# Hash attention and a gelu feed-forward on one core: another order of the start, and a later mark for GpSimd's sums

## The chip, the cores and the metric

The kernel runs on one core of a Trainium2 chip. Its engines have instruction streams of their own: TensorE (PE, with its weight loads as PEld), VectorE (DVE), ScalarE (ACT), GpSimd (POOL) and SyncE (SP). SP and ACT issue most of the transfers. The metric is the device time in microseconds of one execution.

## The reference

Two blocks follow each other. First attention over 4 batches of 8 heads, 768 positions, 64 elements a head, in which a query sees only the keys that fall in its own bucket; the bucket is the six signs of the row times a projection. Then a feed-forward block over the 3072 tokens.

```python
q_bits = (np.einsum('bhsd,dk->bhsk', q, proj) > 0).astype(np.int64)
k_bits = (np.einsum('bhsd,dk->bhsk', k, proj) > 0).astype(np.int64)
mask = q_bucket[:, :, :, None] == k_bucket[:, :, None, :]
scores = np.where(mask, scale * np.matmul(q, k.transpose(0, 1, 3, 2)), -1000000000.0)
attn = np.exp(scores - max);  attn = attn / (sum + 1e-09)
x = np.matmul(attn, v)          # heads side by side: 3072 x 512
h = x @ w_in                    # 512 -> 2048
g = h * (1.0 / (1.0 + np.exp(-1.702 * h)))
out = g @ w_out                 # 2048 -> 512
```

The inputs q, k, v and proj are float32; the two weights are float64 and are turned into float32 on the chip.

## The kernel before, in words

**Order.** The instructions of TensorE, VectorE, ScalarE and GpSimd keep the order in which the program writes them (`manual_schedule`, line 72). Only SP's transfers are placed by the framework: a transfer of SP goes ahead as early as its tile and its semaphores allow. Transfers on ACT and GpSimd stand in those engines' own order.

**Attention** (lines 286 to 618) goes over 16 pairs of heads (4 batches, 4 pairs). For a pair it has q and k turned (features on the partitions), and sign features of the bucket bits as bfloat16. `scores` (426) makes for each of 6 key tiles one product of features, which puts a large negative number where the buckets differ, and one float32 product of q and k into the same PSUM bank; ScalarE takes the exponential. `add_low` on GpSimd and `add_high` on VectorE add the exponentials for the denominators; `values` (453) multiplies by v; `total`, `invert` and `norm` divide.

**The first pair** (`first_pair`, 345) has its own path, as nothing is there to hide its loads. SP and ACT ask for half of k each, then for the projections `pj` (two copies, on partitions 0 to 63 and 64 to 127, line 357), then for q. TensorE warms with four products of a zero tile `idle` (362). `hash_weights` (123) makes hash weights of `pj` on VectorE: four small products for k and one copy into the padded `pf0`, then the same for q. `turned` (365) turns half of k or q by products with `ident` into a PSUM tile `tp`, which VectorE or ScalarE copies to kT or qT. `bits` (373) makes the signs of one half: a product with `pf0` into PSUM (`hash0`), and a comparison on VectorE into the features kf or qf. `measure` (396) sums squares on ScalarE, for a guard. The order is: turn k first half, k second half, q first half, q second half; bits of k first half, q first half, k second half; then the first scores; the bits of the second half of q come behind the first three key tiles. The PSUM tiles of `tp` and `hash0` come from the pool of the scores, which has three buffers.

**Conversion of w_in** (`convert`, 158). Chunks of 512 columns come in as raw float64 bits (`raw`, 512 KB each, one buffer), and VectorE and ScalarE make float32 of them, one chunk in each pair's iteration from pair 2 on. `begin` (517) makes a chunk's generator and asks for its transfer; `step` (514) goes on with it. The helper `behind` (316) is a memset of one column on VectorE: a transfer into that tile then waits for it.

**Feed-forward** (698 on). Both products use seven-product block schemes (Strassen-Winograd), nested once, so that sums of operand quarters stand ahead of the products and sums of results behind them. The second product has 21 output steps (`steps_out`, 1022: three blocks of tokens by seven outer products). In an output step `product_of_halves` (1066) makes seven products of halves, 2 x 4 float32 passes of 256 columns each, in the order 1, 2, 3, 6, 7, 5, 4, and VectorE adds them up. Four operand sums of the next step, `g_sums` (1044: t1, t2, d12, t4), run on VectorE between those additions. The sums of w_out's quarters, `inner_sums` (1015), run on GpSimd, for the first seven steps alone. Their start is held by `mark`, a copy of one element on GpSimd, in steps 2, 3, 5 and 6 (1233): GpSimd goes on when that element has been written. In the trace the L1077 products of steps 1, 2, 3 and 4 start at 605.90, 617.99, 630.08 and 642.65 us.

The lines of the change:

## Time and profile before

| | us |
|---|---|
| median of 3 runs | 859.48 |
| lowest and highest | 858.7, 860.01 |
| the profiled execution | 858.67 |
| its span | 856.8 |
| TensorE busy | 846.2 |
| VectorE busy | 703.3 |
| GpSimd busy | 353.4 |
| ScalarE busy | 344.9 |
| first scores' product starts | 10.80 |
| last product ends | 848.3 |

The page gives busy times by engine, the chain of work that ended last, and groups of instructions. A row of the order of time has start, duration, engine, line, operation, result and operands, shape and count, and in brackets the engine's idle time before it and what ended it. A float32 matmul appears as two records, one for each pass.

### The profile page before, as it was taken

How to read it: one execution, taken by the hardware profiler on the slowest of the kernel's cores; microseconds unless marked ns; L12 is line 12 of the kernel's file. 1: busy time of each engine (PE TensorE's matmuls, PEld its weight loads, DVE VectorE, ACT ScalarE, POOL GpSimd, SP SyncE). 2: the span in 40 equal slices, each digit the busy share in tenths (PEclk: the TensorE clock that was granted, in tenths of full speed). 3: DMA queues.
4: the chain of work that ended last, by engine and by line, in shares of the span. 5: the costliest groups of instructions: out<-in, count | busy, mean ns of one | idle time of the engine just before them, and what ended most of it. 6: DMA issues, size and time to landing. Idle time of an engine off the chain costs nothing.

```text
span 856.8 us, 13648 instructions
## 1 busy us (share of the span) xinstructions
PE 846.2 (99%) x5007; PEld 529.2 (62%) x5007; DVE 703.3 (82%) x1072; ACT 344.9 (40%) x549; POOL 353.4 (41%) x316
## 2 busy tenths in 40 slices
PE   9999999999999999999999999999999999999996
PEld 4444444444444444566666666545888888888885
DVE  4589999999999885788987788577998977797776
ACT  5866667777666654343444444433000000000000
POOL 4343333433433359996854476669725000000000
PEclk9999999999999999999999999999999999999999
DMA  5625755445563104436555546587745685467524
GB/s 131 101 47 107 113 89 85 85 86 99 115 97 71 47 26 150 144 134 233 194 204 217 221 153 234 202 278 257 275 151 190 192 254 197 155 191 245 197 99 101
DMA packets 160987, 132.11 MB, mean 154 GB/s; under 512 B 122608, under 2 KB 137616, under 8 KB 155536
## 3 DMA queue, kind: packets, MB, share of 16 engines
q1 hardware_dynamic: 152016, 106.63, 45.0%
q10 hardware_dynamic: 8896, 24.53, 8.3%
q8 instruction: 41, 0.67, 0.3%
q14 instruction: 34, 0.28, 0.1%
HBM read 79.69 MB, written 50.33 MB: 152 GB/s over the span
## 4 chain that ended last, share of the span: by engine, by line
PE 96%; DVE 2%; DMA 1%; ACT 0%; issue 0%; ACTq 0%; SPq 0%; DVEq 0%
PE product L1077 28%; PE product L751 22%; PE ps L435 18%; PE av L468 15%; PE small L819 6%; PE product L819 3%; PE dn L489 1%; PE hash L411 1%; DVE xT L1081 1%; DVE y L1057 1%; DMA pj<-in_proj_dram 1%; PE hash L376 0%; DVE v L1081 0%; DVE raw_g L223 0%; DVE t2a L224 0%
## 5 line engine op out<-in xcount | busy, mean ns | idle before, releaser
L436 ACT ACTIVATE e<-ps 128x768 f32<-128x768 f32 x192 | 151.2, 812 | 25.7 <-PE ps L435 23.1
L435 PE MATMUL ps<-qT,kT 64*128 64x384 f32 x768 | 155.1, 482 | 0.0
L443 POOL TENSOR_TENSOR acc<-e 128x768 f32<-128x768 f32 x32 | 51.8, 1617 | 193.8 <-ACT e L436 174.3
L468 PE MATMUL av<-e,v 128*32 128x385 f32 x1536 | 128.0, 487 | 0.0
L751 PE MATMUL product<-xT,w_in_sb 128*128 128x512 f32 x216 | 100.1, 593 | 0.1
L468 PEld LDWEIGHTS av<-e,v 128*32 128x32 f32 x1536 | 48.5, 109 | 76.2 <-issue 74.6
L435 PEld LDWEIGHTS ps<-qT,kT 64*128 64x128 f32 x768 | 68.0, 187 | 38.5 <-issue 38.4
L751 PE MATMUL product<-t_x,s_in 128*128 128x512 f32 x192 | 89.4, 592 | 0.0
L1090 ACT COPY u<-product 128x256 f32<-128x256 f32 x21 | 7.8, 372 | 172.2 <-PE product L1077 139.0
L751 PEld LDWEIGHTS product<-xT,w_in_sb 128*128 128x128 f32 x216 | 40.9, 190 | 36.5 <-issue 33.0
L435 PE MATMUL ps<-qf,kf 64*128 64x384 bf16 x384 | 62.9, 324 | 0.1
L444 POOL TENSOR_TENSOR acc<-acc,e 128x768 f32<-128x768 f32 x32 | 55.8, 1744 | 2.5
L751 PEld LDWEIGHTS product<-t_x,s_in 128*128 128x128 f32 x192 | 36.5, 190 | 29.7 <-issue 26.8
L449 DVE SCALAR_TENSOR_TENSOR acc<-e 128x768 f32<-128x768 f32 x32 | 47.7, 1490 | 5.1 <-ACT e L436 5.1
L767 DVE TENSOR_TENSOR u<-product,u 128x256 f32<-128x256 f32 (+1 forms) x60 | 28.4, 486 | 16.4 <-PE product L819 13.2
L435 PEld LDWEIGHTS <-kf 64*128 64x128 bf16 x384 | 18.9, 94 | 35.1 <-issue 6.2
L451 DVE TENSOR_TENSOR acc<-acc,e 128x768 f32<-128x768 f32 x32 | 34.3, 1072 | 3.3
L451 DVE TENSOR_TENSOR acc<-acc,acc 128x768 f32<-128x768 f32 x32 | 31.2, 974 | 6.3 <-POOL acc L444 3.2
L1077 PE MATMUL product<-raw_g,xT 128*128 128x256 f32 x152 | 35.1, 379 | 0.0
L222 POOL TENSOR_TENSOR u<-v,u 128x1024 f32<-128x1024 f32 (+1 forms) x11 | 23.9, 2168 | 21.9 <-ACT v L764 8.1
L767 DVE TENSOR_TENSOR v<-product,v 128x512 f32<-128x512 f32 x24 | 16.5, 689 | 19.4 <-PE product L751 19.4
L767 DVE TENSOR_TENSOR c<-small,c 128x256 f32<-128x256 f32 (+1 forms) x54 | 24.1, 460 | 8.8 <-PE small L819 8.6
(278 smaller groups left out, 1727.3 us busy)
## 6 DMA issues: line engine op xcount, KB each, us to landing
raw_g<-g_dram SPq DMA_DIRECT2D x22, 1024.0 KB
s_in<-g_dram SPq DMA_DIRECT2D x20, 1024.0 KB
g_dram<-c ACTq DMA_DIRECT2D x18, 512.0 KB
raw<-in_moe_w_out_dram ACTq DMA_DIRECT2D x16, 512.0 KB
raw<-in_moe_w_in_dram SPq DMA_DIRECT2D x15, 512.0 KB
v<-in_v_dram SPq DMA_DIRECT2D x32, 192.0 KB
k<-in_k_dram SPq DMA_DIRECT2D x60, 96.0 KB
q<-in_q_dram SPq DMA_DIRECT2D x60, 96.0 KB
```

What stands on the lines that cost most here:

```text
L222: return [lambda: eng.tensor_tensor(t1, b12, b11, op=Alu.subtract), lambda: eng.tensor_tensor(b12, b22, b12, op=Alu.subtract), lambda: eng ...
L435: nc.tensor.matmul(ps[:, j, 0:HS], a[hs, keys], m[hs, cols], start=not last, stop=last)
L436: nc.scalar.activation(es[c][:, kt, :, 0:HS], ps[:, :, 0:HS], Act.Exp, scale=1.0 / D**0.5)
L443: nc.gpsimd.tensor_tensor(acc, es[c][:, 0, :, 0:HS], es[c][:, 1, :, 0:HS], op=Alu.add)
L444: nc.gpsimd.tensor_tensor(acc, acc, es[c][:, 2, :, 0:HS], op=Alu.add)
L449: nc.vector.scalar_tensor_tensor(acc, e[0], T * TINY, e[1], op0=Alu.add, op1=Alu.add)
L451: nc.vector.tensor_tensor(acc, acc, x, op=Alu.add)
L468: nc.tensor.matmul(av[D * j + d : D * j + d + 32, :], vt[:, t, j, d : d + 32], es[c][:, t, j, :], start=(t == 0), stop=(t == T - 1))
L751: nc.tensor.matmul(ps, wq[LEFT[i]][:, kc, :], xq[RIGHT[i]][:, kc, :], start=(start and kc == 0), stop=(kc == K2 - 1), skip_group_check=not ...
L767: nc.vector.tensor_tensor(dst, x, y, op=Alu.add)
L819: nc.tensor.matmul(x, wq[LEFT[i]], xq[RIGHT[i]], start=start, stop=True, skip_group_check=True)
L1077: nc.tensor.matmul(ps, wq[LEFT[i]][:, c, :], gq[RIGHT[i]][:, c, :], start=(c == 0), stop=(c == F4 - 1))
```

## The change

Four edits:

- The projections are asked for first of all in the program, by two transfers on GpSimd's queue, ahead of GpSimd's making of `ident`. The tile `idle` and its memset are gone; the warming products read a constant 1.0 in float32, of 256, 256, 256 and 128 columns.
- The first chunk's transfer is put behind a memset of `raw` on VectorE, which stands behind the features of pair 3. On SP it moves from behind the first loads of v to behind the feature writes of pair 3, ahead of the loads of k and q for pair 5.
- In the first pair, the first half of kT is copied by ScalarE instead of VectorE. The bits of both halves of k come first, then those of q's first half; the second half of q is turned behind them. The sum of squares of q moves ahead of the copy of that half on ScalarE. The `hash0` tiles of q come from another PSUM pool (`mps`).
- In the output steps 2 and 3 `mark` copies an element of t2 of that step, instead of an element of the results of the step before.

```diff
-    idle = const.tile([P, 512], BF16, name="idle")
-    nc.vector.memset(idle, 0.0)
+    pj = const.tile([P, NB], F32, name="pj")
+    for j in range(2):
+        nc.gpsimd.dma_start(out=pj[D * j : D * (j + 1)], in_=proj)
     ident = const.tile([P, P], F32, name="ident")
     make_identity(nc, ident)
...
-    def convert(cv, dst, src, queue=None, psum=None):
+    def convert(cv, dst, src, queue=None, psum=None, behind=None):
         raw = cv.tile([P, CW, 2], U32, tag="raw", name="raw")
+        if behind is not None:
+            behind(raw[:, 0, 0:1])
         (queue or loader[0]).dma_start(out=raw, in_=src)
...
-                    if i == 0:
-                        for j, queue in enumerate((nc.sync, nc.scalar)):
-                            queue.dma_start(out=pj[D * j : D * (j + 1)], in_=proj)
...
-                for _ in range(4):
-                    nc.tensor.matmul(aps.tile([P, 512], F32, tag="av", name="warm"), idle[:, 0:P], idle, start=True, stop=True)
+                for cols in (256, 256, 256, P):
+                    one = [nc.const_aps.tensor(1.0, [P, x], F32) for x in (P, cols)]
+                    nc.tensor.matmul(aps.tile([P, cols], F32, tag="av", name="warm"), *one, start=True, stop=True)
...
-                    h = sps.tile([P, 2, 512], F32, tag="s", name="hash0")[:, 0, 0:HS]
+                    if name == "q":
+                        h = mps.tile([P, HS], F32, tag="m", name="hash0")
+                    else:
+                        h = sps.tile([P, 2, 512], F32, tag="s", name="hash0")[:, 0, 0:HS]
...
-                turned("k", 0, nc.vector.tensor_copy)
+                turned("k", 0, nc.scalar.copy)
                 turned("k", 1, nc.vector.tensor_copy)
                 turned("q", 0, nc.scalar.copy)
-                turned("q", 1, nc.scalar.copy)
                 measure(0, "q")
                 bits("k", 0)
+                bits("k", 1)
                 bits("q", 0)
-                bits("k", 1)
+                turned("q", 1, nc.scalar.copy)
                 return lambda: bits("q", 1)
...
-                    conv[n] = convert(cv, *in_chunks[n - 2])
+                    conv[n] = convert(cv, *in_chunks[n - 2], behind=behind if n == 2 else None)
...
-                    nc.gpsimd.tensor_copy(mark, ms[OUTER[n - 1]][0:1, 0, 0:1])
+                    nc.gpsimd.tensor_copy(mark, (g_quarters(n)[5] if n < 4 else ms[OUTER[n - 1]])[0:1, 0, 0:1])
```

More of the change, by code (lines that the diff above doesn't have):

```diff
@@ L82 @@
     later = []
-    pj = const.tile([P, NB], F32, name="pj")
     def offsets(name, row):
```

## The prediction

> **What bounds the kernel now.** I read the page first (busy time, chain), then the chain at the start, the rows of the first pair's transposes, and the order of time around the one place where TensorE waits late.

> ```profile
> span 856.8 us, 13648 instructions
> PE 846.2 (99%) x5007; PEld 529.2 (62%) x5007; DVE 703.3 (82%) x1072; ACT 344.9 (40%) x549; POOL 353.4 (41%) x316
> PE 96%; DVE 2%; DMA 1%; ACT 0%; issue 0%; ACTq 0%; SPq 0%; DVEq 0%
> ```

> TensorE is the bound nearly everywhere: 846.2 of 856.8 us, 96% of the chain. An edit can pay only where TensorE stands still, or where it does filler. That leaves the start (first scores at 10.80 us), the tail behind the last product (848.3 to 856.8 us by VectorE and the last stores, not touched), and small holes. The chain of waits at the start:

> ```profile
> 1.20 4.38 DMA pj<-in_proj_dram
> ...
> 6.27 0.18 DVE pf_k L133
> ...
> 6.95 0.18 DVE pf_q L133
> 7.14 0.48 DVE kT L371
> 7.61 0.04 issue
> 7.66 0.88 PE tp L369 x12
> 8.54 1.50 PE hash L376 x4
> ...
> 10.13 0.63 DVE qf L377
> 10.76 0.04 issue
> 10.80 2.60 PE ps L435 x18
> ```

> Read it downwards: the projections, two transfers of 1.5 KB asked for at 1.20, land at 5.58 and hold VectorE. Eight small products and two copies into the weights (1.45 us) stand between them and the copies of kT. The last q transposes wait for the first copy to free their PSUM buffer (7.61), the hashes stand behind those transposes, and qf ends at 10.76. The page of one tile gives TensorE's two speeds:

> ```profile
> L369 PE MATMUL tp<-ident,k x24: 420/421/474, 3.8 to 6.3; 128*64 128x128 f32 x24
> L369 PE MATMUL tp<-ident,q x24: 272/273/472, 6.5 to 8.3; 128*64 128x128 f32 x24
> ```

> The same form takes 421 ns until 6.3 us and 273 ns after. By starts, 24 passes of k last 2.9 us (107 ns apart), and 12 of q 0.88 us (55 ns apart): the array runs at half rate up to about 6.5 us. The granted clock reads 1.00 all along, so only durations show it. Last, the order of time in the second half:

> ```profile
> 629.17 1.26 DVE L1081 TENSOR_TENSOR v<-v,xT 128x256 f32<-128x256 f32 x1
> ...
> 630.23 1.33 POOL L217 TENSOR_TENSOR w_in_sb<-xT,w_in_sb 128x512 f32<-128x512 f32 x1
> 630.36 1.95 DVE L1081 TENSOR_TENSOR xT<-xT 128x256 f32<-128x256 f32 x2
> ...
> 634.35 1.22 DVE L224 TENSOR_TENSOR t2b<-s_in,t1b 128x1024 f32<-128x1024 f32 x1
> ...
> 635.67 1.53 PE L1077 MATMUL product<-t2b,w_in_sb 128*128 128x256 f32 x6 [0.25 <-issue]
> ```
> ```profile
> 639.86 0.43 DVE L1081 TENSOR_TENSOR v<-v,xT 128x256 f32<-128x256 f32 x1
> ```

> The same addition takes 1.26 us beside POOL's sums and 0.43 without them. t2b comes at 635.57, and TensorE, which wanted it at 635.26 (starts 1.73 apart per product), begins at 635.67.

> **The change, part by part.** The sum is made against the profiled execution: 858.67 us, a span of 856.8 and 1.87 around it. That lies 0.81 below the median of the runs shown (859.48).

> *POOL's sums behind t2 (steps 2 and 3).* Nothing is added but a later wait. In step 2 the mark waited for the sum c11 (613.59) and its four sums ran from 613.7 to 619.1; in step 3 they ran from 626.3 to 631.6. Three additions between SBUF tiles took 1.41, 1.49 and 1.38 us there in step 2, and 1.26 and 1.49 in step 3, for 0.43 alone. Behind t2 these 2.9 and 1.9 us go, and t2b comes at about 633.7 or before, ahead of 635.26. TensorE gets back 0.41 us (635.67 less 635.26) and up to 0.07 of restart: I take 0.45, with 0 and 0.48 as ends. Queued behind the mark on POOL are the four sums, of which the later output step has need from 633.5 and 646.1 on. They would end at about 626 and 639, before both. What VectorE does next to them is late next: d12 and t4, alone 1.22 us, up to 2.28 beside POOL (the longest such row, t1b at 652.86). d12 of step 3 ends then by 636, for a product at 637.0; t4 by 638.7, for 640.5. Both are covered, by 1 us and more.

> *The start.* Projections: two transfers move from the two hardware queues to POOL's, ahead of ident. The ACT and SP queues lose 0.57 and 0.59 us of issue each, so q is asked for 0.6 us sooner (it was not late by more than that: first transpose of q at 6.46, when k's had ended). POOL has no transfer in this trace. Nearest rows: an issue takes 0.40 to 0.82 us on SP, and landing took 3.1 us (k: issue 0.73, first use 3.81) to 4.38 (pj). So pj lands between 0.73+0.8+3.1 = 4.6 and 0.73+1.64+4.38 = 6.75. I take 5.0, nearer to the first, as no other packets stand in that queue. It has to be there 0.78 us (the products for k) before the first hash. POOL's other memsets move back by 0.8 to 1.6: ident ended at 1.30 and is first used behind the warming; above_q ended at 2.94 and is used at 9; the last ended at 8.55, and POOL then idled 4.97 us. Hidden.

> Warming: 4 x 512 columns in bfloat16 become 896 columns in float32, started without a memset: about 0.85 instead of 1.19. By the hash rows, 384 columns in float32 take 0.645 us at full rate, so 896 take 1.5, or 3.0 at half rate. The four waits between cost 0.2 each (a warming product took 0.63, of which 0.43 is streaming at half rate). It ends at about 4.65, and k's transposes, at 3.81 before, start 0.85 later: this is a cost, paid back only because the old chain waited for pj anyway.

> From there TensorE works without a hole: 24 passes of k, 12 of q, three hashes (3 x 0.645), 0.16 of drain, 0.62 of qf with 0.1 of signals; the last q transposes run under qf. kT's first half goes to ACT (0.48), which has finished measuring k at 4.81, so no copy holds a hash. If the rate doubles at 6.5 as before: k until 6.9, q until 7.55, hashes until 9.5, scores at 10.4, against 10.80: 0.4 gained. If it doubles at 5.0, since TensorE starts sooner and is denser: k until 6.15, q until 6.8, hashes until 8.75, scores at 9.65: 1.15 gained. If it doubles at 8.0: scores at 11.1, 0.3 lost. I take 0.65, between the first two.

> [...]

> *First chunk later.* Its transfer moves on SP from 3.86 us to behind the feature writes that end at 63.0, ahead of the loads of k and q issued at 63.12 to 67.54. From rows: issue to landing 3.1 us (k, at the start) to 4.4, so 66.2 to 67.5; VectorE wants it at 67.37. At worst 0.1 late for six instructions whose results TensorE does not need for 200 us. The loads behind it come up to 2.5 us later (landed by 72.5, first used by VectorE at 80.1). One memset of 0.06 is added on VectorE. Taken at 0, ends 0 and 0.3. Without the slack at 80 it would cost its 2.5.

> Sum: 858.67 - 0.45 - 0.65 = 857.57, say **857.6**.

> **The rivals.**
> 1. *The warming eats the gain.* If the float32 weight loads (0.19 each at full rate) are not hidden, warming ends near 5.9 and scores start at about 11: the start loses 0.2, t2 still gives 0.45, so 858.4. Half-rate work until 8.0 gives the same, 858.5. For it: the warming ends after k has landed. Against it: loads lie under products everywhere else in this trace.
> 2. *Everything pays.* The rate doubles during the warming: 1.15 and 0.48, 857.0. For it: denser work, earlier. Against: the old warming, 2.5 us long, did not do it.
> 3. *POOL's queue is slow (slower than before).* The place is VectorE's wait for pj. Scores start 0.78+1.94+0.16+0.75 = 3.6 us behind pj's landing, so from 7.2 on the start loses, and from 9.4 on the whole is slower by over 0.2%; a landing at 10 gives 861.0. For it: no row bounds POOL's transfers, and ident stands behind their issue. Against: the rows' upper end is 6.75. [...]
> 4. *Nothing shows.* t2 was late only in this execution and the start is bound elsewhere: 858.7.

> **How the numbers follow.** Forecast 0.50, rival 1 0.20, rival 2 0.14, rival 3 0.11, rival 4 0.05. About 0.2% (1.7 us) is what a measurement of this kernel can tell from no change. The forecast is 0.22% under the median, 0.12% under the profiled execution, so it falls on either side of that line: I give three fifths of it to faster. Faster 0.30 + 0.14 = 0.44; within 0.20 + 0.20 + 0.05 = 0.45; slower 0.11. The range goes from rival 2 less 0.3 for the free instant of the clock, 856.7, to rival 1 with the median's 0.81 above its profile and the 0.5 by which runs lie above that, 859.8.

> **What would show it.** In the changed kernel's profile: pj from POOL landing before about 6; k's transposes starting at 4.5 to 4.9; three hashes in a row, and first scores at 9.6 to 10.5; additions next to the mark in steps 2 and 3 at 0.43 us; no idle time before the product that reads t2b; d12 or t4 longer than 1.22, with nobody waiting. Wrong it would be if the warming reaches past 5.5, if pj comes after 7, or if TensorE has a new hole between 620 and 645, or at 78 to 90, where the late loads are used.

## The result, and the profile after

| | before | after |
|---|---|---|
| median of 7 runs each, us | 858.71 | 861.81 |
| lowest and highest | 858.13, 860.01 | 860.97, 862.76 |
| ratio after / before, 95% interval | | 1.0033, 1.0021 to 1.0044 |
| profiled execution, its span | 858.67, 856.8 | 860.98, 859.1 |

The changed kernel is slower by 0.33%, outside the range of the prediction (856.7 to 859.8). The medians differ by 3.10 us, the two profiled executions by 2.30; that of after lies 0.83 below its median. The page of after:

```profile
span 859.1 us, 13660 instructions
PE 848.0 (99%) x5011; PEld 530.7 (62%) x5011; DVE 701.7 (82%) x1071; ACT 345.8 (40%) x550; POOL 359.6 (42%) x318
PE 96%; DVE 2%; ACT 0%; issue 0%; ACTq 0%; DVEq 0%
```

The page looks like that of before: TensorE is the bound, and the busy times of TensorE, VectorE and ScalarE moved by 2 us or less (GpSimd's by 6.2). The 2.3 us are found by laying TensorE's products of both traces beside each other, in order, and noting where the difference of their starts changes:

| place in the changed kernel | difference there, us | sum |
|---|---|---|
| first scores, 11.61 instead of 10.80 | +0.81 | 0.81 |
| product dn of the second pair (50.45 before), behind VectorE's additions | +0.49 | 1.30 |
| a product at 410.95 | -0.08 | 1.22 |
| product that reads t2b in step 3 (635.67 before) | -0.50 | 0.72 |
| last product's end to the span's end, 10.09 instead of 8.51 | +1.58 | 2.30 |

Only the fourth line is what the prediction counted on. The order of time at the start, with the rows of TensorE's weight loads (PEld) and products (PE), and one row each of ScalarE and VectorE that tell when k and the projections were there:

```profile
0.75 0.50 PEld L359 LDWEIGHTS warm<-const-float32-1.0 128*128 128x128 f32 x2 [0.75 <-issue]
0.78 4.60 PE L359 MATMUL warm<-const-float32-1.0 128*128 128x256 f32 x8 [0.78 <-PEq L1319]
...
2.03 0.50 PEld L359 LDWEIGHTS warm<-const-float32-1.0 128*128 128x128 f32 x2 [0.78 <-PE warm L359]
...
3.31 0.50 PEld L359 LDWEIGHTS warm<-const-float32-1.0 128*128 128x128 f32 x2 [0.78 <-PE warm L359]
...
3.93 0.84 ACT L401 ACTIVATE junk<-k 128x768 bf16<-128x768 f32 x1 [0.76 <-DMA k<-in_k_dram]
...
4.59 0.50 PEld L359 LDWEIGHTS warm<-const-float32-1.0 128*128 128x128 f32 x2 [0.78 <-PE warm L359]
...
5.17 0.23 DVE L127 SCALAR_TENSOR_TENSOR pf_k<-pj,ones 64x6 f32<-64x6 f32 x2 [3.34 <-DMA pj<-in_proj_dram]
...
5.32 2.73 PE L366 MATMUL tp<-ident,k 128*64 128x128 f32 x24
```

A float32 product has two weight loads. A pair of them takes 0.50 us here, at half rate, and by the brackets each pair waits for the product ahead of it: 0.50 of loads and 0.78 of streaming, 1.28 us for each product of 256 columns. The warming ends at 5.38; k, as ScalarE shows, has been there since 3.93.

The second place, the order of time on VectorE, first before, then after:

```profile
40.92 0.95 DVE L449 SCALAR_TENSOR_TENSOR acc<-e 128x768 f32<-128x768 f32 x1
41.97 0.96 DVE L451 TENSOR_TENSOR acc<-acc,e 128x768 f32<-128x768 f32 x1
```
```profile
41.79 0.95 DVE L449 SCALAR_TENSOR_TENSOR acc<-e 128x768 f32<-128x768 f32 x1
43.27 0.96 DVE L451 TENSOR_TENSOR acc<-acc,e 128x768 f32<-128x768 f32 x1 [0.53 <-ACT e L436]
44.33 0.96 DVE L451 TENSOR_TENSOR acc<-acc,acc 128x768 f32<-128x768 f32 x1
```

The bracket names ScalarE's exponentials. But the last exponential that this addition reads had ended by 37.28 (ScalarE's 31st signal), six microseconds earlier. So VectorE stood for 0.53 us for something that no semaphore shows, and the denominators came about that much later to TensorE.

The fourth place, where step 3 reads t2b, first VectorE, then GpSimd, then TensorE:

```profile
631.84 1.21 DVE L223 TENSOR_TENSOR t2b<-s_in,t1b 128x1024 f32<-128x1024 f32 x1
...
634.45 2.09 DVE L224 TENSOR_TENSOR t4g<-s_in,t2b 128x1024 f32<-128x1024 f32 x1
```
```profile
633.12 1.11 POOL L1235 COPY mark<-t2b 1x1 f32<-1x1 f32 x1 [4.84 <-DVE t2b L223]
634.19 1.26 POOL L213 TENSOR_TENSOR w_in_sb<-xT 128x512 f32<-128x512 f32 x1
```
```profile
634.74 1.89 PE L1077 MATMUL product<-s_in,w_in_sb 128*128 128x256 f32 x8
636.47 1.89 PE L1077 MATMUL product<-t2b,w_in_sb 128*128 128x256 f32 x8
```

t2b is written by 633.05, 3.4 us ahead of its product, GpSimd's sums start behind it, t4 is the long row now, and TensorE has no idle time there.

For the last place I read the transfers' view of the stretch behind the last product. It has 40 equal slices, and each digit is the busy share of the DMA engines in tenths; first before (848.3 to 856.8), then after (849.0 to 859.1):

```profile
DMA  6517999998999988999999999984000001000000
```
```profile
DMA  6419999889998999999999810100000000200000
```

Before, the DMA engines are busy at eight tenths and more from 0.9 to 5.5 us behind the last product, and the last stores are done at 6.15. After, nearly all is done at the same distance, and some 30 packets straggle until 7.51. SP, which waits for the stores, makes its last branch at 8.44 instead of 6.99.

### The profile page after: what moved, and what is told of

Its sections match the earlier page's. It is cut to its first block, busy times and chain, and to the rows that moved or that the text cites. A ratio compares the mean times of both kernels' runs of the same rounds, so it can differ in the third digit from the quotient of the medians.

```text
span 859.1 us, 13660 instructions
## 1 busy us (share of the span) xinstructions
PE 848.0 (99%) x5011; PEld 530.7 (62%) x5011; DVE 701.7 (82%) x1071; ACT 345.8 (40%) x550; POOL 359.6 (42%) x318
## 4 chain that ended last, share of the span: by engine, by line
PE 96%; DVE 2%; ACT 0%; issue 0%; ACTq 0%; DVEq 0%
PE product L1077 28%; PE product L751 22%; PE ps L435 18%; PE av L468 15%; PE small L819 6%; PE product L819 3%; PE dn L489 1%; PE hash L411 1%; DVE xT L1081 1%; DVE y L1057 1%; PE warm L359 1%; PE tp L366 0%; PE hash L376 0%; DVE v L1081 0%; DVE raw_g L222 0%
## 5 line engine op out<-in xcount | busy, mean ns | idle before, releaser
L435 PE MATMUL ps<-qT,kT 64*128 64x384 f32 x768 | 155.1, 482 | 0.0
L435 PEld LDWEIGHTS ps<-qT,kT 64*128 64x128 f32 x768 | 68.0, 187 | 38.6 <-issue 38.6
L435 PE MATMUL ps<-qf,kf 64*128 64x384 bf16 x384 | 62.8, 324 | 0.0
L435 PEld LDWEIGHTS <-kf 64*128 64x128 bf16 x384 | 18.8, 94 | 34.6 <-issue 7.4
L1077 PE MATMUL product<-raw_g,xT 128*128 128x256 f32 x152 | 35.1, 379 | 0.0
L222 POOL TENSOR_TENSOR v<-c,v 128x1024 f32<-128x1024 f32 (+1 forms) x15 | 32.3, 2156 | 1.0
```

The lines of the kernel that those rows point to most:

```text
L222: lambda: eng.tensor_tensor(b12, b22, b12, op=Alu.subtract),
L435: nc.tensor.matmul(ps[:, j, 0:HS], a[hs, keys], m[hs, cols], start=not last, stop=last)
L1077: nc.tensor.matmul(ps, wq[LEFT[i]][:, c, :], gq[RIGHT[i]][:, c, :], start=(c == 0), stop=(c == F4 - 1))
```

## The experiments

All times of the start are from the span's start; "end" is the time from the last product's end to the span's end, and "VectorE's records" are the instructions of VectorE that the trace shows, waits and branches included. The runs of the four sets stood beside runs of before with medians of 859.18, 858.77, 858.95 and 858.70 us.

| kernel | VectorE's records | first scores | last product ends | end | median | ratio to before, 95% |
|---|---|---|---|---|---|---|
| before | 1479 | 10.80 | 848.29 | 8.51 | | |
| after | 1477 | 11.61 | 849.01 | 10.09 | 861.81 | 1.0033, 1.0021 to 1.0044 |
| e1 | 1477 | 10.98 | 848.30 | 9.80 | 860.94 | 1.0020, 1.0010 to 1.0029 |
| e2 | 1477 | 12.46 | 849.79 | 9.77 | 862.09 | 1.0033, 1.0022 to 1.0045 |
| e3 | 1478 | 10.84 | 848.13 | 10.09 | 859.70 | 1.0004, 0.9994 to 1.0013 |
| e4 | 1479 | 11.89 | 849.29 | 8.83 | 859.48 | 1.0000, 0.9989 to 1.0011 |
| p1 | 1479 | 12.20 | 849.12 | 8.68 | 859.49 | 1.0006, 0.9997 to 1.0016 |
| p2 | 1479 | 10.63 | 847.55 | 8.35 | 858.17 | 0.9992, 0.9982 to 1.0001 |
| p3 | 1478 | 11.91 | 849.30 | 10.21 | 860.22 | 1.0019, 1.0009 to 1.0029 |
| p4 | 1480 | 10.68 | 848.07 | 8.36 | 858.88 | 1.0004, 0.9994 to 1.0013 |
| b1 | 1479 | 10.49 | 847.40 | 8.84 | 858.51 | 0.9989, 0.9981 to 0.9998 |
| b2 | 1479 | 10.95 | 847.87 | 8.48 | 858.10 | 0.9988, 0.9980 to 0.9997 |
| b3 | 1479 | 10.43 | 847.92 | 8.54 | 858.33 | 0.9990, 0.9981 to 0.9999 |
| b4 | 1479 | 10.86 | 848.24 | 8.32 | 858.61 | 0.9994, 0.9985 to 1.0003 |
| x1 | 1480 | 10.69 | 848.23 | 8.49 | 858.60 | 0.9998, 0.9989 to 1.0007 |
| x2 | 1479 | 10.81 | 847.72 | 8.47 | 858.05 | 0.9994, 0.9985 to 1.0003 |

### First set: which part makes the start and the end late

e1 is the changed kernel with another warming:

```diff
-                for cols in (256, 256, 256, P):
-                    one = [nc.const_aps.tensor(1.0, [P, x], F32) for x in (P, cols)]
+                for cols in (512, 512, 512, 512):
+                    one = [nc.const_aps.tensor(1.0, [P, x], BF16) for x in (P, cols)]
```

> The changed kernel with four warming products of 512 columns of a bfloat16 constant instead of the float32 ones; all else as changed. Theory (the changed kernel's first scores are late by 0.81 us because four float32 products, at half rate and with weight loads of 0.50 us that are not hidden, end at 5.38 and not at 3.8): warming ends at about 3.3, k's transposes start when k has landed, at about 3.9, first scores at 10.1 to 10.5 (11.61 in the changed kernel), and the whole is 1.1 to 1.5 us shorter than the changed kernel, near 860.4 (median of the changed kernel's runs 861.8). Rival (not the warming, but the time at which TensorE's rate doubles, sets the scores): transposes start at 3.9 but run at half rate until 7.5, first scores at 11.1 to 11.6, time within 0.5 us of the changed kernel's.

Warming ended at 3.28, k's transposes started at 4.07, first scores came at 10.98: 0.63 sooner than in the changed kernel, and the ratio fell from 1.0033 to 1.0020, about 1.1 us. The theory has the direction; its 10.1 to 10.5 missed, because the rate doubled only at 7.7, as the rival has it. TensorE then stood idle for 0.8 us between warming and k. Both count.

e2 is the changed kernel with the projections back on the SP and ACT queues:

```diff
-    for j in range(2):
-        nc.gpsimd.dma_start(out=pj[D * j : D * (j + 1)], in_=proj)
...
+                    if i == 0:
+                        for j, queue in enumerate((nc.sync, nc.scalar)):
+                            queue.dma_start(out=pj[D * j : D * (j + 1)], in_=proj)
```

> The changed kernel with the projections asked for where they were before, by the SP and ACT queues behind k; no transfer by GpSimd is left. Theory (a program that uses GpSimd's queue ends later: in the changed kernel 10.09 us lie between the last product's end and the span's end, for 8.51 before): the end takes 8.4 to 8.7 us again and the time is about 1.6 us below the changed kernel's, 860.2. Rival (the longer end is chance, a few straggling packets of the last stores): the end takes anything from 8.5 to 10, without regard to the queue, and the time stays within 0.5 us of the changed kernel's. First scores: within 0.3 of 11.61 by both, since the projections would land at about 5.6 and VectorE would have the hash weights by 7.1, ahead of the first hash at 8.6.

The end stayed long, at 9.77, and the time at 862.09: GpSimd's queue is not what makes the end long, and the theory fell. First scores came at 12.46, as TensorE ran at half rate into the first hash at 9.35 (0.55 us between that hash's two passes, 0.33 to 0.43 elsewhere).

e3 is before with the mark alone:

```diff
-                    nc.gpsimd.tensor_copy(mark, ms[OUTER[n - 1]][0:1, 0, 0:1])
+                    nc.gpsimd.tensor_copy(mark, (g_quarters(n)[5] if n < 4 else ms[OUTER[n - 1]])[0:1, 0, 0:1])
```

> The kernel before with the later mark in output steps 2 and 3 alone. Theory (this part does what the prediction said and nothing else): TensorE's wait of 0.25 us before the product that reads t2b in step 3 goes, the work behind it starts 0.4 to 0.5 us sooner, the time is 858.2 beside 858.7, ratio 0.9994. Rival (t2b was late by chance in one execution, or VectorE's next sums become late and give it back): no difference in the end of the last product, ratio 1.0000.

At the product that reads t2b it won 0.44 us against before, as the theory says. Yet the median is not better, and the end took 10.09. In its profile dn, the product of the second place, came 0.25 later too, though VectorE did not stand at that addition: its transpose of q ahead waited 2.99 us for the load (1.74 in before). That product has no slack: lateness of VectorE there showed at dn both times (0.49 in after, 0.25 in e3). The rival that the long end is chance now looked no better either: it had come in four kernels of four with the later mark, and in none of two without.

e4 is before with the projections by GpSimd alone:

```diff
+    pj = const.tile([P, NB], F32, name="pj")
+    for j in range(2):
+        nc.gpsimd.dma_start(out=pj[D * j : D * (j + 1)], in_=proj)
...
-    pj = const.tile([P, NB], F32, name="pj")
...
-                    if i == 0:
-                        for j, queue in enumerate((nc.sync, nc.scalar)):
-                            queue.dma_start(out=pj[D * j : D * (j + 1)], in_=proj)
```

> The kernel before with one edit: the projections asked for first by GpSimd's queue, in place of the SP and ACT queues. Theory (GpSimd's queue costs at the program's end): first scores at about 10.2 to 10.8, as the hash weights no longer wait for the projections; between the last product's end and the span's end 9.9 to 10.2 us instead of 8.51; time 859.6 to 860.3, ratio 1.001 to 1.002. Rival (the longer end is chance): the end takes 8.5 us, time 858.2 to 858.7, ratio 0.999 to 1.000.

The end was 8.83: again not GpSimd's queue. The first scores, at 11.89, missed both expectations. VectorE in e4:

```profile
5.40 0.23 DVE L132 SCALAR_TENSOR_TENSOR pf_k<-pj,ones 64x6 f32<-64x6 f32 x2 [3.29 <-DMA pj<-in_proj_dram]
7.02 0.24 DVE L132 SCALAR_TENSOR_TENSOR pf_k<-pj,ones 64x6 f32<-64x6 f32 x2 [1.39 <-DMA pj<-in_proj_dram]
```

The second half of the projections came at 7.0. The last of its packets ended at 6.64, in the changed kernel at 5.14. What stands ahead in e4 and not in the changed kernel is the first chunk, 512 KB asked for by SP at 2.61. So two parts of the change may belong together: with the chunk asked for early, the projections by GpSimd lost here (that the chunk is the cause is not shown; no run tried it alone).

### Second set: the borders of VectorE's program

What the kernels with a long end share need not be the mark itself: VectorE's number of records is 1477 or 1478 in them, and 1479 in those with a short end. The mark in t2 takes one wait out of VectorE's records, the tile idle took a memset, the copy of kT moved to ScalarE, and the chunk's memset was added. Counting VectorE's records from 0, the standstill at 42.8 is at record 63. Standstills of 0.40 us that no semaphore explains recur at distances of 128 records or multiples of it; record 63 and every 128th behind it are called borders here. The table has the time from the end of the record ahead to the start of the one named; "none" is where the two overlap:

| record | 63 | 191 | 319 | 959 | 1087 | 1471 |
|---|---|---|---|---|---|---|
| before, us | none | 0.04 | 0.04 | 0.40 | 0.40 | none |
| after, us | 0.47 | 0.40 | 0.40 | none | 0.73 | 0.42 |

At 959 and 1087 VectorE was still at work on earlier instructions for part of that time or all of it, so little of it is idle time. Over all sixteen kernels, 60 such places have a wait, a branch or a register load ahead: 50 of them show 0.40 to 0.47 us (three 0.73), the other ten, all at record 1343, nothing. Of the 132 places with an ordinary instruction ahead none shows it.

The page lists two queues of the kind instruction; the packets of one of them (q14, 34 of them in the span of before) are of 8192 bytes, those of the other (q8) of 16384. The packets of q14 come where the standstills are: behind 29 of the 45 standstills ahead of record 1471 a packet of this queue starts 0.66 to 0.96 us after VectorE goes on (behind the other 16, all at record 1087, 3.1 to 3.9 us after). So the standstills are read here as VectorE's wait for its own program; that is the author's reading, as no record shows such a wait. Record 1471 is, before, the load of the guard's value into a register; after it is a wait behind VectorE's first branch. The next kernels move the borders without touching what the engines do.

p1, the changed kernel with two memsets of one element:

```diff
     nc.vector.memset(ones, 1.0)
+    for i in range(2):
+        nc.vector.memset(const.tile([1, 1], F32, name=f"pad{i}"), 0.0)
```

> The changed kernel with two more VectorE instructions, memsets of one element at the start, where VectorE has nothing to do. Theory (VectorE reads its program in blocks of 128 instructions; the changed kernel has two fewer VectorE instructions than before, so that two block borders come to stand right behind a wait, and VectorE stands 0.4 to 0.5 us there: at 42.8 us, and at the last branch): with the old count both standstills go. At about 43 us the additions into acc follow without idle time and TensorE's product dn at 50.5 starts 0.45 to 0.5 earlier against the first scores; the end from the last product to the span's end is 8.4 to 8.9 us (10.09 in the changed kernel); the time is 1.7 to 2.0 below the changed kernel's, near 860.0. Rival (the later end comes from POOL's sums behind t2 or from the new order, and the count of instructions means nothing): 10 us of end and the changed kernel's 861.8, if not 0.1 more for two more instructions.

Two instructions more, and the ratio falls from 1.0033 to 1.0006, with intervals that do not touch. VectorE of p1 around 43 us, as the theory says:

```profile
42.30 0.95 DVE L451 SCALAR_TENSOR_TENSOR acc<-e 128x768 f32<-128x768 f32 x1
43.36 0.96 DVE L453 TENSOR_TENSOR acc<-acc,e 128x768 f32<-128x768 f32 x1
44.42 0.96 DVE L453 TENSOR_TENSOR acc<-acc,acc 128x768 f32<-128x768 f32 x1
```

No idle time is left, dn starts no later than the scores did, and the end is 8.68. The traffic behind its last product (849.1 to 857.8) has no straggling packets:

```profile
DMA  7526999998999989999999999980000010000100
```

p2, before with the mark (as in e3) and one memset, and p3, before without the tile idle:

```diff
             def begin(n):
+                if n == 8:
+                    nc.vector.memset(const.tile([1, 1], F32, name="pad"), 0.0)
...
```

> The kernel before with the later mark, and one VectorE memset of one element in the eighth iteration of attention, so that VectorE's count of instructions is that of before. Theory (block borders): the last product ends 0.4 to 0.5 us before that of the kernel before, from step 3 of the output, and the end takes 8.4 to 8.9 us (10.09 with the mark alone); time 858.6 to 858.8 beside 859.2, ratio 0.9994 to 0.9996. Rival (the later mark itself makes the end longer, by where it leaves POOL's sums): end of 9.8 to 10.1 us, time 859.7, ratio 1.0004 or above.

End 8.35, time 858.17: the mark's gain stands once the count is kept. At the product reading t2b it won 0.50 against before.

```diff
-    idle = const.tile([P, 512], BF16, name="idle")
-    nc.vector.memset(idle, 0.0)
...
-                for _ in range(4):
-                    nc.tensor.matmul(aps.tile([P, 512], F32, tag="av", name="warm"), idle[:, 0:P], idle, start=True, stop=True)
+                for cols in (512, 512, 512, 512):
+                    one = [nc.const_aps.tensor(1.0, [P, x], BF16) for x in (P, cols)]
+                    nc.tensor.matmul(aps.tile([P, cols], F32, tag="av", name="warm"), *one, start=True, stop=True)
```

> The kernel before, whose warming products read a bfloat16 constant instead of the tile idle; idle and its memset on VectorE are gone, which makes VectorE's program one instruction shorter. Nothing near the end is touched. Theory (block borders): VectorE's first branch at the end stands 0.4 us late, the end takes 9.7 to 10.1 us instead of 8.51, and the time is 1.0 to 1.5 above before, 860.4, unless the start gives something back (warming starts 0.4 sooner; first scores 10.3 to 11.5, as the clock falls). Rival (the end is set by the mark or is chance): an end of 8.5 us, time 858.9 to 859.3.

An edit in the first microsecond made the end 10.21 instead of 8.51. The time rose by 1.45 against before. The start was also late (scores at 11.91), as q landed late, at 7.5, and the rate doubled at about 8.7.

p4, before with the later first chunk alone:

```diff
+        if behind is not None:
+            behind(raw[:, 0, 0:1])
...
-                    conv[n] = convert(cv, *in_chunks[n - 2])
+                    conv[n] = convert(cv, *in_chunks[n - 2], behind=behind if n == 2 else None)
```

> The kernel before with the first chunk's transfer put behind a memset on VectorE, as in the change, and nothing else. Theory (this part costs nothing, and one instruction more on VectorE moves the last border to a transpose that nothing waits for): no new hole of TensorE between 62 and 90 us, end 8.4 to 8.9 us, time 859.0 to 859.4, ratio 1.000. Rival (the later loads of k and q behind it cost, or the chunk itself comes late): a hole of 0.3 to 2.5 us at 67 to 90 us, ratio 1.0005 to 1.003.

No new hole of TensorE, end 8.36, ratio 1.0004 (0.9994 to 1.0013): this part costs nothing that shows.

### Third set: the parts with the borders kept

b1, the changed kernel with the warming of before and one memset for the count (so the projections, the order, the chunk and the mark remain):

```diff
+    idle = const.tile([P, 512], BF16, name="idle")
+    nc.vector.memset(idle, 0.0)
...
+    nc.vector.memset(const.tile([1, 1], F32, name="pad"), 0.0)
...
-                for cols in (256, 256, 256, P):
-                    one = [nc.const_aps.tensor(1.0, [P, x], F32) for x in (P, cols)]
-                    nc.tensor.matmul(aps.tile([P, cols], F32, tag="av", name="warm"), *one, start=True, stop=True)
+                for _ in range(4):
+                    nc.tensor.matmul(aps.tile([P, 512], F32, tag="av", name="warm"), idle[:, 0:P], idle, start=True, stop=True)
```

> The changed kernel with the warming of before (the zero tile idle, four bfloat16 products) and one more VectorE memset, so that VectorE's count is that of before. What differs from before is then the early projections by GpSimd, the order of the hashes, the later chunk and the later mark. Theory (float32 warming alone made the start late, the other parts of the start pay what the prediction said): TensorE's rate doubles at 6.5 to 7.5, as in all kernels with the zero tile, first scores at 10.3 to 10.6, last product 0.7 to 0.9 us before that of before, end 8.4 to 8.9, time 858.0 beside 858.8, 0.2 below the kernel with mark and pad alone. Rival (the order of the hashes gains nothing where TensorE has no hole, since the same 48 transposes and three hashes stand ahead of the scores): first scores at 10.7 to 11.2, time 858.3 to 858.8, at or above the kernel with mark and pad alone.

First scores at 10.49 and 858.51: faster than before, 0.9989 (0.9981 to 0.9998). Against p1 (1.0006) only the warming differs: by the medians of each beside its own runs of before, -0.44 and +0.72, float32 warming costs about 1.2 us. Against the mark alone (b2) the other parts bring nothing that shows.

b2 is p2 once more:

> The kernel before with the later mark and one VectorE memset in the eighth iteration, once more with more rounds, beside the others of this call. Theory: the gain is 0.45 to 0.5 us at step 3 of the output, ratio 0.9993 to 0.9996. Rival (the 858.17 measured before came from chance): ratio 1.000.

0.9988 (0.9980 to 0.9997), with 0.48 won at the product that reads t2b. The mark gains; its size in the runs (0.85) lies above the 0.48 of the trace, within the interval.

b3, before with the order of the hashes and one memset:

```diff
+    nc.vector.memset(const.tile([1, 1], F32, name="pad"), 0.0)
...
+                    if name == "q":
+                        h = mps.tile([P, HS], F32, tag="m", name="hash0")
...
-                turned("k", 0, nc.vector.tensor_copy)
+                turned("k", 0, nc.scalar.copy)
                 turned("k", 1, nc.vector.tensor_copy)
                 turned("q", 0, nc.scalar.copy)
-                turned("q", 1, nc.scalar.copy)
                 measure(0, "q")
                 bits("k", 0)
+                bits("k", 1)
                 bits("q", 0)
-                bits("k", 1)
+                turned("q", 1, nc.scalar.copy)
```

> The kernel before with the order of the hashes, ScalarE's copy of kT's first half and the mps tiles for q's hashes, as changed, and one VectorE memset so that VectorE's count stays. Projections, warming, chunk and mark as before. Theory (the order pays where VectorE has the weights late): first scores at 10.3 to 10.6, ratio 0.9995. Rival (nothing gained, since the same work of TensorE stands ahead of the scores): first scores at 10.7 to 11.1, ratio 1.0000 to 1.0005.

First scores at 10.43, 0.9990 (0.9981 to 0.9999), as the theory says; but in this execution the rate doubled at 5.8, sooner than in any other, and x2 below is needed to read it.

b4, before with six warming products of a constant, up to k's landing:

```diff
-    idle = const.tile([P, 512], BF16, name="idle")
-    nc.vector.memset(idle, 0.0)
...
+    nc.vector.memset(const.tile([1, 1], F32, name="pad"), 0.0)
...
+                for cols in (512, 512, 512, 512, 512, 512):
+                    one = [nc.const_aps.tensor(1.0, [P, x], BF16) for x in (P, cols)]
```

> The kernel before with six warming products of 512 columns of a bfloat16 constant 1.0, from 0.78 us to the landing of k at about 4.2, without idle; one VectorE memset keeps VectorE's count. Theory (what put off the doubling of TensorE's rate to 7.7 and 8.6 with four such products was the idle time of 0.8 us behind them): without that gap the rate doubles at 6.5 to 7.0 or sooner, first scores at 10.3 to 10.9, time within 0.3 of before. Rival (the constant itself, or the instant in each execution, puts it off): doubling at 7.5 or later, first scores at 11.3 to 12, time 0.5 to 1 above before.

The rate doubled at about 6.1, where four such products with idle time behind them had it at 7.7 and 8.7 (e1, p3). So the constant itself does not put it off, and the theory of the gap is borne out, by one execution. The time shows no gain (0.9994, 0.9985 to 1.0003). TensorE of e1, with the gap in the bracket:

```profile
0.78 2.50 PE L359 MATMUL warm<-const-bfloat16-1.0 128*128 128x512 bf16 x4 [0.78 <-PEq L1319]
4.07 2.91 PE L366 MATMUL tp<-ident,k 128*64 128x128 f32 x24 [0.78 <-POOL above_q L110]
```

### Fourth set: how 0.4 us became 1.5, and the sum

x1, before with a needless memset of 128x1024 behind VectorE's last transpose:

```diff
     whole(ff)
+    nc.vector.memset(t_x[:, 0], 0.0)
     fixed.close()
```

> The kernel before with one VectorE instruction more behind its last transpose, a memset of 128x1024 in a tile that nobody needs any more, so that VectorE reaches its last branch 0.3 to 0.5 us later, while its blocks' borders stay harmless. It tells apart how 0.4 us of standstill became 1.5 us of end. Theory 1 (VectorE's lateness at the branch is what counts: its jump then meets the other engines' jumps and the last stores): end of 9.8 to 10.2 us, time 1.3 to 1.6 above before. Theory 2 (what counts is that the fetch of VectorE's next block, seen 0.44 us behind the last product in every kernel with a short end, comes late; the standstill only goes with it): the fetch at 0.44 is there, the end 8.4 to 8.9 us, or at most the 0.4 later, and the time within 0.4 of before.

VectorE's last branch came 3.30 us behind the last product, as late as in the changed kernel (3.31; before 2.93), and the end was 8.49. So its lateness is not the cause. The packets on the instruction queue of 8192 bytes, by time behind the last product (and how long each took, us):

```
before  0.44 (0.31)  4.77 (0.31)  5.68 (0.48)  7.23 (0.40)  8.19 (0.31)
after                4.61 (0.71)  5.31 (0.50)  5.65 (0.48)  8.63 (0.46)  8.70 (0.44)
x1      0.43 (0.31)  4.66 (0.31)  5.98 (0.31)  7.09 (0.36)  8.26 (0.51)
```

In all eleven kernels with an end under 8.9 one packet stands at 0.42 to 0.45; in all five with an end of 9.77 or more it is missing there, and three packets instead of two meet the last stores. With 1 or 2 records fewer ahead of it, the border at record 1471 is reached only among the last waits and branches (in after it starts at 852.23 us, between branches at 851.76 and 852.32); 27 to 34 packets of the stores then end later than 6.3 us behind the last product, in all five kernels, and none does in the eleven. What a packet of instructions there does to the stores (which DMA engine, in which order) the traces do not tell; that stays open.

x2, before with the order and the mark, and two memsets for the count:

> The kernel before with the order of the hashes and the later mark of the change, and two VectorE memsets (one at the start, one in the eighth iteration) that keep VectorE's count; projections, warming and chunk as before. Theory (both parts pay, each in its place): first scores at 10.2 to 10.6, 0.4 to 0.5 more from step 3 of the output, last product at 847.3 to 847.6, end 8.4 to 8.9; time 857.7 to 858.0 beside 858.9, ratio 0.9986 to 0.9990. Rival (the start differs with the instant at which the rate doubles alone): no better than the mark alone, 858.1 to 858.3, ratio 0.9990 to 0.9993.

First scores at 10.81 (the rate doubled at 7.4), 0.49 won at t2b by the trace, 858.05, 0.9994 (0.9985 to 1.0003). The rival is nearer: no better than the mark alone. What the order of the hashes is worth by itself stays open: b3 is faster than before, x2 not faster than b2, and the instant of the doubling (5.8 and 7.4) differs by more than either. Two profiles with the doubling at 7.4 show no gain: first scores at 10.69 in x1 with the old order, at 10.81 in x2 with the new one, whose transposes of k started 0.13 later. The fastest kernels by their medians are b2 and x2, before with the later mark and VectorE's count kept: 858.10 and 858.05, which their intervals do not tell apart.

## Why the prediction was wrong

*POOL's sums behind t2: right.* The term was 0.45 between 0 and 0.48; nine profiles show 0.44 to 0.50. The additions beside the mark, d12 and t4 came as described: t4 took 2.09 (the prediction's bound was 2.28), and nobody waited for it.

*The start: wrong in two steps.* "It ends at about 4.65" is the first: the warming ended at 5.38. The products, 896 columns in all, were costed by streaming, 3.0 us, and 0.2 for each of the waits; what was missed is that a pair of float32 weight loads took 0.50 at half rate and lay open, four times. Rival 1 had this, with 5.9 and scores at 11, and a chance of 0.20; the scores came at 11.61, later than it says, because of the second step: "the rate doubles at 6.5 as before". By the prediction's own rows, a warming up to 5.38, with the doubling still at 6.5, puts the scores at 10.7, which takes back nearly all of the 0.65; the doubling at 7.7 on top puts them at 11.3. Of the rest 0.25 lies at the first hash, which starts 0.20 behind the last transpose and has 0.43 between its passes, where the sum had steady distances. The granted clock of the profile, 1.00 throughout, does not show the doubling; by the passes' distances (107 against 55 ns, read to about 0.1 us) the rate doubled at:

| what TensorE did before k | kernels | doubled at, us |
|---|---|---|
| four products of the zero tile, up to 3.7, 0.1 to 0.4 idle | before, e3, e4, p2, p4, b1, b2, b3, x1, x2 | 5.8 to 7.6 |
| six products of a constant, up to 4.56 | b4 | 6.1 |
| four products of a constant, up to 3.28, 0.8 to 0.9 idle | e1, p3 | 7.7, 8.7 |
| four float32 products with open loads, up to 5.38 | after, p1, e2 | 7.7, 9.0, about 9.5 |

In before itself the first passes of q still took up to 472 ns, so its doubling lies at 6.7 to 6.8 rather than 6.5. The instant does vary from one execution to the next, by 1.8 us within one kind of warming, and by these draws it was later on top behind a thin or interrupted warming: the five such kernels have it at 7.7 or later, the eleven others at 7.6 or before. Why it was, and what else sets the instant, no run here shows. That the rate would double at 5.0 because TensorE starts sooner and is denser was the author's estimate, and no profile has the doubling before 5.8. The 0.3 in the range "for the free instant of the clock" no run shows either; the runs showed doublings from 5.8 to about 9.5. Half-rate work until 8.0 was in the prediction as one case of the start, 0.3 lost, and in rival 1; the 0.65 was taken between the other two cases.

A third step was built on one draw: the projections "land at 5.58 and hold VectorE". In the profile of before that landing made the hash weights ready at 7.14. That is the latest of the eleven kernels with the projections on SP's and ACT's queues: the others have them at 5.64 to 6.94. By GpSimd's queue they were ready at 6.88 to 7.13 (four kernels), and at 8.23 in e4. The later of the two landings came at 4.26 to 5.37 in those ten kernels, and by GpSimd's queue at 5.65 to 5.89 (6.99 in e4): that queue brought the projections later, not sooner. That "no other packets stand in that queue" did not make them early: in the changed kernel the last packet ended at 5.14 and the landing came at 5.65, where the sum took 5.0. And without the late landing the new order saves nothing: it puts a third hash (0.645) ahead of the first scores in place of twelve transposes (12 x 55 ns, 0.66).

*First chunk later: right*, by p4.

*What the sum did not have: the program's own reading.* That the tail is "not touched" is the step that failed most: +1.58 of the 2.30. A further +0.49 came from the standstill at 42.8, far from any edit. Both came from VectorE's program being two records shorter, and both went with two idle memsets (p1). That the change makes VectorE's program shorter can be read off the diff; the prediction gave it no term. The traces show the price: 0.40 to 0.47 us (three times 0.73) at 50 of 60 borders where the record ahead is a wait, a branch or a register load, nothing at the 132 others, and an end of 9.77 to 10.21 instead of 8.32 to 8.84 where the border falls among the last branches. What a branch does they do not show apart from what a wait does.

The slower outcome had a chance of 0.11, all of it on GpSimd's queue (rival 3), which was not the cause.

## What to carry to other kernels

When an edit changes the number of VectorE's instructions, even by one, the places 128 records apart at which VectorE stood 0.40 to 0.47 us here move along the whole kernel (other engines were not tried): compare two kernels' ends (here 8.32 to 8.84 and 9.77 to 10.21) and unexplained standstills before blaming the edit, and try one or two idle instructions (p1: from 1.0033 to 1.0006). A wait whose semaphore had its value long ago is no wait for that engine (in after, the 0.53 us put down to ScalarE, whose exponentials had ended six microseconds earlier). A term that rests on the instant of one execution (a landing, with hash weights ready at 5.64 to 7.14; the doubling of TensorE's rate, at 5.8 to 7.6 with one kind of warming) needs several profiles. By the draws here the doubling came at 7.7 or later when the filler that warms TensorE left 0.8 us idle ahead of the real work or had open weight loads.
